# Attention with hashed masks, a gated product layer and eight experts on one core: key parts, row writes, a weight split and gates in other places

## The chip, the cores and the metric

The kernel runs on one core of a Trainium2 chip. The core has five engines, each with its own queue of instructions, worked off in order: TensorE (PE in the rows, its weight loads PEld), VectorE (DVE), ScalarE (ACT), GpSimd (POOL) and SyncE (SP, which here only issues transfers). They wait for each other by semaphores. The metric is device microseconds (us) of one execution; less is better.

## The reference

Three layers follow one another. The attention (2 batches, 8 heads, 768 rows, head width 64) lets a query see only keys of its own bucket, where a bucket is the six signs of a projection; the gated layer multiplies two products of its input and maps them back; the last layer sends each row to the one expert of eight with the largest logit.

```python
q_bits = (np.einsum('bhsd,dk->bhsk', q, proj) > 0).astype(np.int64)
k_bits = (np.einsum('bhsd,dk->bhsk', k, proj) > 0).astype(np.int64)
mask = q_bucket[:, :, :, None] == k_bucket[:, :, None, :]
scores = np.where(mask, scale * np.matmul(q, k.transpose(0, 1, 3, 2)), -1000000000.0)
attn = softmax(scores); x = np.matmul(attn, v)          # then rows of 512, 1536 of them
y = (x @ w_a) * (x @ w_b) @ w_out                       # 512 -> 1536 -> 512
xn = y / (np.linalg.norm(y, axis=-1, keepdims=True) + 1e-06)
logits = xn @ en.T / tau; expert_idx = np.argmax(logits, axis=1)
out[mask] = gate_w[mask, None] * (np.maximum(y[mask] @ w1[e], 0.0) @ w2[e])   # for each e
```

## The kernel before

Everything is written in the order in which it is to run; each engine gets its share of that order, and nothing is sorted anew afterwards.

**Attention** (`attention`, from L70). Work goes in 48 units of 256 query rows of one head, three to a head; two heads share their tiles (a pair). In a unit TensorE makes two score tiles (`st`, L205 and the masks' part L208), VectorE takes the row maximum (`nm`, L213), ScalarE exponentiates (`e`, L219), GpSimd scales (L232), VectorE transposes in blocks (`et`, L239). The first two units of a head, s = 0 and 1, each do half of the value products of the head two before it (`pv`, L248), into four banks (`pvb`), two for each half of the rows. In the third, s = 2, these banks are emptied by ScalarE (`xp`, `co`, L268) and are then used for the next pair: in one kind of head for the transposes of raw keys and queries (`turned`, L114), which ScalarE copies out (`k`, `q`, L128), in the other kind for their projections (`signs`, L163 and L181), of which ScalarE takes the signs (`sk`, `qf`, L154). From the key signs two masks are made (`kf`, L143, by `masks`). Both kinds fill the key's banks in the middle of the unit (`fresh`) and the query's at its end. The functions that empty them are kept in `preps` and called in the next unit, behind its first exponential and behind `masks()`. The value products of that next unit write the same banks.

Weight steps of the gated layer are hung into units by a table (`plan`, `places`): each of six jobs has seven steps, among them a GpSimd addition (L465), a VectorE guard (`late`, L476) and a last split into a rounded part (ScalarE, L481) and its rest (GpSimd, L482).

**Gated layer and router.** From there on there is one list, `main`, of TensorE's pieces: `p` are six products of the gated layer (`ab`, L551), after the last of four of which VectorE multiplies (`a`, L564), ScalarE rounds (`g`, L565) and GpSimd takes the rest (L566); `o` are six products back (`yp`, L583), whose sums VectorE adds into `y` (L588). `after` hangs a job behind a named piece, `chain` a list of jobs behind successive pieces. L is the last of the six chunks of that layer; the pieces of its groups 0 and 1 feed the first batch (rows 0 to 5 of twelve), of groups 2 and 3 the second.

The router's steps are such jobs. `route_in` (T) writes a row block of `y` out (`ybuf`, L646, from SyncE), squares it (`sq`, L653) and transposes it (`yt`, L656). `group_logits` (GL) makes the logits of three blocks (`lgt`, copied by ScalarE to `lgs`, L686), `group_turn` (GT) turns them (`lgu`, L694). The tile of `lgs` and that of the squares are the same single buffer. `route_norm` (`nrm`), `route_choose` (L715 to L729), `route_places` (`pos`, L737), `route_slots` (`slots`, L774) and `gather` (L838) find and fetch the rows of each expert; `route_gates` (VectorE L792 to L802, with an exponential on ScalarE, L793) and `route_gate_slots` (`gates`, L809) give the weights. ScalarE loads a table before that exponential and before the square root of `nrm`.

The experts' weights come by `fetch_expert` and are split by `split_expert` into a rounded part (ScalarE, L832) and its rest (GpSimd or VectorE, L833). `transpose_in` (`xgt`, L854) turns gathered rows; `hidden_rows` (`hr`, L895), `hidden_turn` (`ht`, L910) and `expert_out` (`op`, L927) are the first expert's products. The small products of the router and all transposes there share two banks (`rt`).

Of the kernel before, what the change touches and what calls it, by code (L numbers as in the profile page):

```python
# [25 lines left out]
class Kernel:  # L26
# [37 lines left out]
    def attention(self, xh, xl, pools, hook):  # L64
        nc = self.nc
# [237 lines left out]
        preps = signs(0, 1), signs(0, 0)  # L303
# [4 lines left out]
        preps = []  # L308
# [6 lines left out]
        for u in range(NU + 2):  # L315
            i, r = divmod(u, 6)
            s, w = u % 3, u - 2
            act, last, tr = u < NU, 0 <= u - 1 < NU, w >= 0
            done, fin = divmod(u - 11, 6) if u >= 11 else (-1, 0)
            new = len(pairs)  # L320
            if u == 1 or s == 2 and r == 5:
                new, kind = 1 if u == 1 else (u + 7) // 6, turned
            elif u == 3 or s == 2 and u > 2:
                new, kind = 1 if u == 3 else i + 1, signs
            fresh = []
            if act:
                rowmax(u, 0)
                scores(u, 1)
            moves = [((u - 8) // 3, g) for g in (1, 0)] if s == 2 and u >= 8 else []
            for m in moves[:2 if u == NU - 1 else 1]:  # L330
                epilogue(*m)
            if moves and new < len(pairs):
                fresh.append(kind(new, 1))
            if act:
                expo(u, 0)
            for m in moves[2 if u == NU - 1 else 1:]:
                epilogue(*m)
            masks()
            for prep in preps:
                prep(nc.scalar)  # L340
            if preps and held_kind is turned and held + 1 < len(pairs):
                load(held + 1)
            preps = []
            if u + 1 < NU:
                scores(u + 1, 0)
            if last:
                recip(u - 1)
                normal(u - 1)
            if tr:
                turn(w, 0)  # L350
            hook(u, 3)
            if act:
                rowmax(u, 1)
            if tr:
                turn(w, 1)
            if act:
                expo(u, 1)
            if new < len(pairs):
                preps, held, held_kind = fresh + [kind(new, x) for x in (1, 0)[len(fresh):]], new, kind
            elif s < 2 and u >= 6:  # L360
                pv((u - 6) // 3, range(12 * s, 12 * s + 12))
            hook(u, 0)
            if s == 1 and u >= 7 and (u - 1) // 3 < 2 * len(pairs):
                load_v((u - 1) // 3)
            hook(u, 1)
            if done == len(pairs) - 2:
                for g in range(3):
                    if fin == 2:
                        finish_add(done, cols[g])
            else:  # L370
                for start, step, args in finish:
                    done, fin = divmod(u - 11 - start, 6)
                    if fin == 0 and 0 <= done < len(pairs) - 2:
                        step(done, *args)
            hook(u, 4)
# [39 lines left out]
class Experts:  # L415
# [226 lines left out]
    def route_in(self, i):  # L642

        nc = self.nc
        b, c = divmod(i, self.TB)
        nc.sync.dma_start(  # L646
            out=self.ybuf[b].rearrange("(p c) d -> p c d", c=self.TB)[:, c], in_=self.y[:, i]
        )
        if c == 0:
            self.ss[b] = self.small("ssq", [128, self.TB])  # L650
            self.lg[b] = self.small("lg", [128, self.TB, self.E])
        sq = self.sb.tile([128, self.DM], F32, tag="sq", name="sq", bufs=1)
        nc.scalar.activation(sq, self.y[:, i], AF.Square, accum_out=self.ss[b][:, c:c + 1])  # L653
        p = self.rt.tile([128, 512], F32, tag="rt", name="yt")
        for k in range(self.KD):
            nc.tensor.transpose(p[:, k * 128:(k + 1) * 128], self.y[:, i, k * 128:(k + 1) * 128], self.K.ident)  # L656
        t, c = divmod(i, 3)
        if c == 0:
            self.yT[t] = self.sb.tile([128, self.KD, 384], F32, tag="yt", name="yt", bufs=1)
        nc.vector.tensor_copy(  # L660
            self.yT[t][:, :, c * 128:(c + 1) * 128], p.rearrange("p (k s) -> p k s", s=128)
        )
# [383 lines left out]
def tile_kernel(ctx, tc, q, k, v, proj, w_a, w_b, w_out, emb, tau, w1, w2, out, dbg=None):  # L1046
    K = Kernel(tc, q, k, v, proj, w_a, w_b, w_out, emb, tau, w1, w2, out)
    nc = tc.nc
# [3 lines left out]
    with tc.manual_schedule():  # L1052
# [15 lines left out]
        with tc.tile_pool(name="conv", bufs=1, side="left") as X.conv, \  # L1068
                tc.tile_pool(name="att", bufs=2, side="right") as sb, \
                tc.tile_pool(name="ps_s", bufs=2, space=PSUM) as ps_s, \  # L1070
                tc.tile_pool(name="ps_pv", bufs=1, space=PSUM) as ps_pv:

            def spare():
                return X.mid.tile([128, 4 * 384], F32R, tag="g", name="spare")

            def late():
                return sb.tile([128, 2 * S], F32, tag="raw", name="late", bufs=1)

            jobs = [X.load_first(w, f, spare) for f in range(2) for w in range(2)]
            outs = [X.load_first(2, f, late) for f in range(2)]  # L1080


            plan = {(-1, 0): [jobs[0][0], jobs[1][0]], (37, 1): [outs[0][0]], (47, 1): [outs[1][0]]}
            places = (
                (3, 4, 5, 6, 6, 9, 12), (7, 10, 11, 12, 12, 13, 18), (15, 17, 19, 22, 22, 23, 28), (21, 25, 26, 28, 28, 29, 34),
                (42, 43, 43, 44, 44, 44, 45),
            )
            plan[NU + 2, 3] = outs[1][1][:4]
            plan[NU + 2, 4] = outs[1][1][4:6]
            plan[NU + 3, 3] = outs[1][1][6:]  # L1090
            for (_, steps), us in zip(jobs + outs, places):
                for m, u in enumerate(us):
                    plan.setdefault((u, 3 if m in (3, 4, 6) else 4), []).append(steps[m])
            plan[13, 0], plan[19, 0] = [jobs[2][0]], [jobs[3][0]]
            first = [(t, f, w, h) for t in range(2) for f in range(2) for w in range(2) for h in range(2)]


            fill = {41: 2, 44: 2, NU: 2, NU + 2: 2, NU + 3: 2, NU + 4: 6}

            held = []  # L1100

            def hook(u, at):
                if at == 3:
                    while held:
                        held.pop(0)()
                for job in plan.pop((u, at), []):
                    job()
                if at == 0:
                    for n in range(fill.get(u, 0)):
                        t, f, w, half = first.pop(0)  # L1110
                        if half == 0:
                            X.part = K.banks[(2, 0)[n // 2]] if u < NU else K.bank()
                        X.gated_products(0, t, f, w, half, X.part, held if u < NU else None)

            K.attention(X.xh, X.xl, (sb, ps_s, ps_pv), hook)
            assert not plan and not first
# [15 lines left out]
        def after(name, fn, *args):  # L1132
            side.setdefault(name, []).append(lambda: fn(*args))

        def chain(name, jobs, stride=1):

            at = next(i for i, m in enumerate(main) if m[0] == name)
            for job in jobs:
                if job:
                    for fn, *args in (job if isinstance(job, list) else [job]):  # L1140
                        after(main[at][0], fn, *args)
                at += stride
# [69 lines left out]
        L = NCH - 1  # L1212
        after(("p", L, 0, 0, 0, 0), reopen)
        for n in range(4):
            after(("p", L, 1 + n // 2, n % 2, 0, 0), split, 0, n, G)
        after(("p", L, 3, 0, 0, 0), split, 0, 4, G)
        after(("o", L, 2, 1), split, 0, 5, G)
        after(("o", L, 2, 2), split, 0, 6, G)
        after(("o", L, 3, 2), split, 0, 7, G)
        after(("e", 0, 1, 0), X.transpose_in, 1, 0)  # L1220
        after(("e", 0, 1, 1), X.transpose_in, 1, 1)
        for n, at in enumerate((("t", 0, 1, 1), ("e", 0, 1, 1), ("e", 0, 1, 2), ("e", 0, 1, 3))):
# [9 lines left out]
        def begin():  # L1232
# [7 lines left out]
        chain(("o", L, 0, 2), [(T, 0), (T, 1), (T, 2), (GL, 0), (GT, 0)], 2)  # L1240
        chain(("o", L, 1, 2), [
            (T, 3), (T, 4), [(T, 5), (X.route_norm, 0)], (GL, 1), [(GT, 1), (X.route_choose, 0)],
            None, None, None, (X.route_places, 0), None, [(X.route_slots, 0), (X.gather, 0, 0)],
            (X.route_gates, 0), None, None, None, None, None, (X.route_gate_slots, 0),
        ])
        chain(("o", L, 2, 1), [(T, 6), (T, 7), (T, 8), (GL, 2), (GT, 2)])
        after(("p", L, 3, 1, 1, 1), begin)
        after(("o", L, 3, 0), X.transpose_in, 0, 0)
        after(("o", L, 3, 0), X.gather, 1, 0)
# [5 lines left out]
        after(("h", 0, 1, 0), X.route_gates, 1)  # L1255
        after(("e", 0, 0, "half"), X.transpose_in, 0, 1)
        after(("e", 0, 0, 2), X.gather, 1, 1)
        after(("e", 0, 1, 0), X.route_gate_slots, 1)
        after(("h", 1, 0), X.route_most)
        for e in range(2, X.E):  # L1260
            for b in range(B):
# [44 lines left out]
```

## Time and profile before

| | before |
|---|---|
| median of 3 runs | 738.83 us (737.4 to 739.58) |
| profiled execution | 740.01 us |
| its span, first to last instruction | 738.1 us |
| TensorE busy | 706.0 us (96%) |
| VectorE, ScalarE, GpSimd busy | 458.5, 356.7, 441.7 us |
| granted TensorE clock, mean | 0.994 |
| chain that ended last, TensorE's share | 79% |

The attention fills the span up to about 240 us, the gated layer follows up to about 537 us, with the router among its last 50, and the experts fill the rest. A timeline row gives the start and the length in microseconds, the engine, the line of the program and the operation; square brackets at its end give how long the engine was idle just before it and which operation's end released it.

### The profile page before, as it was taken

What the parts mean: (1) busy time and instruction counts of PE and PEld (TensorE: products, weight loads), DVE (VectorE), ACT (ScalarE), POOL (GpSimd) and SP (SyncE); (2) the same over time, 40 slices, a digit from 0 to 9 for tenths busy, and PEclk for the clock granted to TensorE, in tenths of its full rate; (3) what the DMA queues carried; (4) which work ended last, traced back from release to release, by engine and by line L of the source; (5) the groups of instructions that cost most, each with busy time, mean ns of one, the idle gap of its engine ahead of it and who ended that gap; (6) DMA issues with size and microseconds to landing.
All of it is one profiled execution on the core that took longest, in us unless ns stands there. A gap on an engine that the chain in (4) does not pass through costs nothing.

```text
span 738.1 us, 16439 instructions
## 1 busy us (share of the span) xinstructions
PE 706.0 (96%) x6793; PEld 584.3 (79%) x6793; DVE 458.5 (62%) x669; ACT 356.7 (48%) x657; POOL 441.7 (60%) x453
## 2 busy tenths in 40 slices
PE   7799999999989999999999999999999999999996
PEld 4356555555658999999999999998888999889995
DVE  3888988988885654655545536434744855555650
ACT  4677887877674333221221221234436655556551
POOL 1666998988786472662745646634513866556651
PEclk9899999999999999999999999999999999999999
DMA  6954566456233230230311111254250957666510
GB/s 151 189 122 111 135 153 140 93 116 138 50 76 108 76 121 27 63 109 6 110 58 58 57 58 58 105 168 155 66 178 30 293 197 241 222 217 239 208 61 23
DMA packets 68605, 88.31 MB, mean 120 GB/s; under 512 B 28963, under 2 KB 41123, under 8 KB 68528
## 3 DMA queue, kind: packets, MB, share of 16 engines
q1 hardware_dynamic: 64320, 79.49, 37.8%
q0 software_dynamic: 2560, 7.34, 2.6%
q8 instruction: 54, 0.88, 0.5%
q10 hardware_dynamic: 1648, 0.39, 0.3%
q14 instruction: 23, 0.19, 0.1%
HBM read 75.52 MB, written 7.34 MB: 112 GB/s over the span
## 4 chain that ended last, share of the span: by engine, by line
PE 79%; DVE 5%; ACT 5%; issue 4%; DMA 3%; POOL 3%; SPq 0%; POOLq 0%; DVEq 0%; ACTq 0%
PE ab L551 24%; PE yp L583 13%; PE op L927 10%; PE hp L877 9%; PE pv L248 8%; PE st L205 5%; ACT e L219 2%; DVE nm L213 2%; PE part L551 2%; PE hr L895 2%; DMA vr<-in_v_dram 2%; DVE et L239 1%; PE st L208 1%; PE xgt L854 1%; POOL e L232 1%
## 5 line engine op out<-in xcount | busy, mean ns | idle before, releaser
L551 PE MATMUL ab<-xh,w 128*128 128x384 f32 x704 | 185.8, 338 | 0.0
L551 PEld LDWEIGHTS ab<-xh,w 128*128 128x128 f32 x704 | 127.7, 188 | 2.0 <-issue 1.2
L566 POOL TENSOR_TENSOR g<-a,g 128x384 fp32r<-128x384 f32 x48 | 57.2, 1191 | 105.8 <-ACT g L565 105.7
L551 PE MATMUL ab<-xl,w 128*128 128x384 f32 x352 | 118.3, 336 | 0.0
L833 POOL TENSOR_TENSOR w<-raw,w 128x1024 fp32r<-128x1024 f32 x36 | 88.0, 2448 | 33.8 <-ACT w L832 32.7
L219 ACT ACTIVATE e<-st,nm 128x768 f32<-128x768 f32 x96 | 86.5, 902 | 40.8 <-DVE nm L213 20.3
L213 DVE TENSOR_REDUCE nm<-st 128x1 f32<-128x768 f32 x96 | 90.2, 941 | 22.7 <-PE st L208 22.6
L583 PE MATMUL yp<-w,g 128*128 128x512 f32 x432 | 102.9, 390 | 0.0
L232 POOL TENSOR_SCALAR e<-e,s,mc 128x768 f32<-128x768 f32 x96 | 95.0, 998 | 5.4 <-POOL s L230 0.2
L239 DVE STREAM_TRANSPOSE et<-e 128x768 f32<-128x768 f32 x96 | 92.3, 963 | 3.9 <-issue 1.5
L205 PE MATMUL st<-ks,qs 64*128 64x384 f32 x192 | 86.5, 531 | 8.2 <-ACT e L219 7.7
L205 PE MATMUL st<-k,q 64*128 64x384 f32 x192 | 86.6, 532 | 7.9 <-ACT e L219 6.9
L583 PEld LDWEIGHTS yp<-w,g 128*128 128x128 f32 x432 | 80.4, 188 | 14.9
L927 PE MATMUL op<-w,hth 128*128 128x512 f32 x256 | 81.0, 397 | 0.1
L877 PE MATMUL hp<-xgh,w 128*128 128x256 f32 x448 | 80.7, 281 | 0.0
L565 ACT CAST g<-a 128x384 fp32r<-128x384 f32 x48 | 24.7, 515 | 104.9 <-DVE a L564 104.9
L248 PE MATMUL pv<-et,vr 32*64 32x192 f32 x3072 | 71.4, 325 | 3.9 <-ACT q L128 1.6
L248 PEld LDWEIGHTS pv<-et,vr 32*64 32x64 f32 x3072 | 59.8, 130 | 19.4 <-issue 9.7
L833 DVE TENSOR_TENSOR w<-raw,w 128x1024 fp32r<-128x1024 f32 x28 | 64.6, 2308 | 14.9 <-ACT w L832 14.9
L877 PEld LDWEIGHTS hp<-xgh,w 128*128 128x128 f32 x448 | 69.1, 188 | 0.3
L560 ACT COPY a<-ab 128x384 f32<-128x384 f32 x44 | 21.0, 478 | 95.1 <-PE ab L551 93.7
L551 PEld LDWEIGHTS ab<-xl,w 128*128 128x128 f32 x352 | 66.2, 188 | 0.8
(202 smaller groups left out, 1244.3 us busy)
## 6 DMA issues: line engine op xcount, KB each, us to landing
raw<-in_moe_w_dram SPq DMA_DIRECT2D x32, 1024.0 KB, 5.3
vr<-in_v_dram SPq DMA_DIRECT2D x64, 192.0 KB, 4.3
raw<-in_moe_w_a_dram SPq DMA_DIRECT2D x5, 1024.0 KB, 5.1
raw<-in_moe_w_b_dram SPq DMA_DIRECT2D x5, 1024.0 KB, 5.0
raw<-in_moe_w_out_dram SPq DMA_DIRECT2D x5, 1024.0 KB, 5.0
raw<-in_k_dram SPq DMA_DIRECT2D x16, 192.0 KB, 4.7
qs<-q SPq DMA_DIRECT2D x16, 192.0 KB, 3.1
ybuf<-y SPq DMA_DIRECT2D x12, 256.0 KB, 6.1
```

The costliest lines, as they stand in the source:

```text
L205: nc.tensor.matmul(st[:, n, :H2], q[d, ql], k[d], start=True, stop=False, tile_position=(64 * n, 0))
L213: nc.vector.tensor_reduce(NM[u][:, t:t + 1], ST[u, t][:, :, :H2], axis=AX.XY, op=ALU.max, negate=True)
L219: nc.scalar.activation(e, ST.pop((u, t))[:, :, :H2], AF.Exp, bias=NM[u][:, t:t + 1], accum_out=SU[u][:, t:t + 1])
L232: nc.gpsimd.tensor_scalar(E[u, t], E[u, t], r[:, t:t + 1], c[:, t:t + 1], ALU.mult, ALU.add)
L239: nc.vector.transpose(ET[h][:, :, c], E.pop((u, t)).rearrange("p a (b s) -> p (a b) s", s=32))
L248: nc.tensor.matmul(pvb[a // 2][m:m + 64, a % 2, :NC * 32], v[d], et[d, n].rearrange("p c s -> p (c s)"), start=(n < 2), stop=(n >= NB32 - ...
L551: nc.tensor.matmul(p[:, :384], w[:, k, fs], x[:, k, cols], start=(k == 0 and n == 0), stop=(k == self.KD - 1 and n == 2),)
L566: nc.gpsimd.tensor_tensor(gl[:, f], a, f32(gh[:, f]), ALU.subtract)
L583: nc.tensor.matmul(p, g[:, f, rows], w[:, f], start=(n == 0), stop=(n == 5))
L833: eng.tensor_tensor(l, raw, f32(h), ALU.subtract)
L877: nc.tensor.matmul(p[:, :256], w[:, k, fs], x[:, k], start=(n == 0), stop=(n == 3 * self.KD - 1))
L927: nc.tensor.matmul(p, h[:, 2 * n + f, rows], w[:, f], start=(n == 0 and f == 0 and m == 0), stop=(n == 3 and f == 1 and m == 2),)
```

## The change

Seven edits, none of which changes what is computed. The functions that empty the key's banks are called at the end of their own unit, behind its second exponential, where they were called in the next unit together with the query's. The row blocks 9 to 11 are written from ScalarE's queue. In the table of weight steps the guard and the last split of the fifth job stand one unit later. The split of expert 0's piece 4 stands behind the last `p` piece of the layer, seven pieces later. Slots, the gather and the gates of the first batch stand one piece later, and so does the turning of the logits of group 2. The gate slots of the second batch stand ahead of the transpose that shares their place.

```diff
             if new < len(pairs):
-                preps, held, held_kind = fresh + [kind(new, x) for x in (1, 0)[len(fresh):]], new, kind
+                for prep in fresh:
+                    prep(nc.scalar)
+                preps, held, held_kind = [kind(new, x) for x in (1, 0)[len(fresh):]], new, kind
...
         b, c = divmod(i, self.TB)
-        nc.sync.dma_start(
+        (nc.scalar if i >= 2 * self.TB - 3 else nc.sync).dma_start(
...
-                (42, 43, 43, 44, 44, 44, 45),
+                (42, 43, 43, 44, 44, 45, 46),
...
-        after(("p", L, 3, 0, 0, 0), split, 0, 4, G)
+        after(("p", L, 3, 1, 1, 1), split, 0, 4, G)
...
+        after(("e", 0, 1, 0), X.route_gate_slots, 1)
         after(("e", 0, 1, 0), X.transpose_in, 1, 0)
...
-            None, None, None, (X.route_places, 0), None, [(X.route_slots, 0), (X.gather, 0, 0)],
-            (X.route_gates, 0), None, None, None, None, None, (X.route_gate_slots, 0),
+            None, None, None, (X.route_places, 0), None, None, [(X.route_slots, 0), (X.gather, 0, 0)],
+            (X.route_gates, 0), None, None, None, None, (X.route_gate_slots, 0),
         ])
-        chain(("o", L, 2, 1), [(T, 6), (T, 7), (T, 8), (GL, 2), (GT, 2)])
+        chain(("o", L, 2, 1), [(T, 6), (T, 7), (T, 8), (GL, 2), None, (GT, 2)])
...
-        after(("e", 0, 1, 0), X.route_gate_slots, 1)
```

On ScalarE, where a head's third unit passes into the next head's first (the first cycle with signs), the order was this; `e` is an exponential, `sk` and `qf` the key and query signs, `kf` the two masks:

```order
L219 ACTIVATE e,su<-st,nm 128x768
L268 COPY xp<-pv 64x2x6x32
L268 COPY co<-pv 64x2x6x32
L219 ACTIVATE e,su<-st,nm 128x768 x2
L154 ACTIVATE sk<-pv,bias 128x384
L154 ACTIVATE qf<-pv,bias 128x384
L219 ACTIVATE e,su<-st,nm 128x768 x2
L143 ACTIVATE kf<-sk,fac 128x384 x2
```

And now:

```order
L219 ACTIVATE e,su<-st,nm 128x768
L268 COPY xp<-pv 64x2x6x32
L268 COPY co<-pv 64x2x6x32
L219 ACTIVATE e,su<-st,nm 128x768
L154 ACTIVATE sk<-pv,bias 128x384
L219 ACTIVATE e,su<-st,nm 128x768
L143 ACTIVATE kf<-sk,fac 128x384 x2
L154 ACTIVATE qf<-pv,bias 128x384
```

The key signs moved ahead of the next unit's first exponential, and with them the masks, which that unit calls ahead of its query signs.

On VectorE, at the gates of the first batch (`so` ends the slots, `lg` to `th` are the gates, `y` the sums of rows 6 and 7), the order was:

```order
L786 CAST so<-oif 128x8
L792 TENSOR_TENSOR lg<-lg,mx 128x48
L795 TENSOR_REDUCE gt<-lg 128x6
L796 TENSOR_SCALAR gt<-gt 128x6
L797 RECIPROCAL gt<-gt 128x6
L799 TENSOR_TENSOR tg<-oh,gt 128x48
L801 CAST th<-tg 128x6x8
L802 TENSOR_TENSOR th<-tg,th 128x6x8
L564 TENSOR_TENSOR a<-ab,a 128x384
L588 TENSOR_TENSOR y<-yp,y 128x512 x2
```

And now:

```order
L788 CAST so<-oif 128x8
L566 TENSOR_TENSOR a<-ab,a 128x384
L794 TENSOR_TENSOR lg<-lg,mx 128x48
L797 TENSOR_REDUCE gt<-lg 128x6
L798 TENSOR_SCALAR gt<-gt 128x6
L799 RECIPROCAL gt<-gt 128x6
L801 TENSOR_TENSOR tg<-oh,gt 128x48
L803 CAST th<-tg 128x6x8
L804 TENSOR_TENSOR th<-tg,th 128x6x8
L590 TENSOR_TENSOR y<-yp,y 128x512 x2
```

The gates now stand between the layer's last product `a` and the sums; on ScalarE their table load and exponential likewise moved behind the rounding of that product and behind the moved split's rounding.

On TensorE, at the logits of group 2 (`lgt`, turned by `lgu`; `hr` are the first hidden products), the order was:

```order
L684 MATMUL lgt<-yt,enT 32x384 x4
L656 MATMUL yt<-ident,y 128x128 x4
L583 MATMUL yp<-w,g 128x512 x6
L694 MATMUL lgu<-ident,lgs 128x128 x3
L656 MATMUL yt<-ident,y 128x128 x4
L672 MATMUL lgp<-enT,yt 128x8 x4
L895 MATMUL hr<-w,xgh 128x256 x8
L895 MATMUL hr<-w,xgl 128x256 x4
```

And now:

```order
L686 MATMUL lgt<-yt,enT 32x384 x4
L658 MATMUL yt<-ident,y 128x128 x4
L585 MATMUL yp<-w,g 128x512 x6
L658 MATMUL yt<-ident,y 128x128 x4
L674 MATMUL lgp<-enT,yt 128x8 x4
L897 MATMUL hr<-w,xgh 128x256 x8
L897 MATMUL hr<-w,xgl 128x256 x4
L696 MATMUL lgu<-ident,lgs 128x128 x3
```

The turning moved behind the first hidden products, so that `lgs`, whose buffer the next square uses, is read there.

## Rows read from the trace of the kernel before

**Rows 1.** Busy time by stretch: us, PE, PEld, DVE, ACT, POOL (instructions), PEclk, DMA.
```profile
140.00:180.00 40.00, 37.51 (x722) 21.89 (x720) 34.60 (x48) 30.77 (x65) 34.30 (x59) 1.00 0.54 120
520.00:560.00 40.00, 39.76 (x275) 35.46 (x275) 21.95 (x77) 18.39 (x34) 14.22 (x10) 1.00 0.41 124
```

**Rows 2.** The chain of waits, start, length, engine and line, a copy cycle.
```profile
117.92 0.70 ACT k L128
```

**Rows 3.** The timeline of ScalarE, cycles with signs.
```profile
129.39 0.66 ACT L460 ACTIVATE r<-spare 128x512 int32<-128x512 uint32 x1
...
130.82 0.58 ACT L154 ACTIVATE sk<-pv,bias 128x384 bf16<-128x384 f32 x1
131.28 0.59 ACT L154 ACTIVATE qf<-pv,bias 128x384 bf16<-128x384 f32 x1
...
134.33 1.11 ACT L143 ACTIVATE kf<-sk,fac 128x384 bf16<-128x384 bf16 x2
...
155.85 0.90 ACT L219 ACTIVATE e<-st,nm 128x768 f32<-128x768 f32 x1 [0.36 <-DVE r L223]
```

**Rows 4.** The timeline of TensorE, value products behind copies and behind signs.
```profile
119.38 2.21 PE L248 MATMUL pv<-et,vr 32*64 32x192 f32 x96 [0.32 <-ACT q L128]
...
131.98 2.21 PE L248 MATMUL pv<-et,vr 32*64 32x192 f32 x96
```

**Rows 5.** The timeline of VectorE, the guard in unit 44.
```profile
207.54 1.21 DVE L476 SCALAR_TENSOR_TENSOR late<-late 128x512 f32<-128x512 f32 x1 [1.09 <-POOL late L465]
```

**Rows 6.** The timeline of all engines, first choice; last row, the second slots.
```profile
516.20 2.40 POOL L833 TENSOR_TENSOR w<-raw,w 128x1024 fp32r<-128x1024 f32 x1
...
516.34 2.32 DVE L721 TENSOR_TENSOR eq<-eq,em 128x48 f32<-128x48 f32 x1
...
519.20 0.20 PE L737 MATMUL pos<-ohb,tri 128*128 128x56 bf16 x1 [0.76 <-DVE ohb L727]
...
521.56 1.10 PE L774 MATMUL slots<-tl,sel 128*128 128x16 f32 x6
...
548.70 0.73 PE L774 MATMUL slots<-tl,sel 128*128 128x16 f32 x6
```

**Rows 7.** The timeline of all engines, gates of the first batch to row 6.
```profile
522.31 1.28 ACT L793 ACT_TABLE_LOAD   x1
...
524.70 2.89 PE L583 MATMUL yp<-w,g 128*128 128x512 f32 x12
...
525.19 0.55 DVE L564 TENSOR_TENSOR a<-ab,a 128x384 f32<-128x384 f32 x1
...
526.19 1.05 ACT L832 CAST w<-raw 128x1024 fp32r<-128x1024 f32 x1
526.26 0.69 DVE L588 TENSOR_TENSOR y<-yp,y 128x512 f32<-128x512 f32 x1 [0.52 <-PE yp L583]
...
527.36 4.74 POOL L833 TENSOR_TENSOR w<-raw,w 128x1024 fp32r<-128x1024 f32 x2
527.42 0.60 PE L656 MATMUL yt<-ident,y 128*128 128x128 f32 x4
```

**Rows 8.** The timeline of all engines, second logits to second place products.
```profile
537.22 0.63 ACT L653 ACTIVATE sq<-y 128x512 f32<-128x512 f32 x1 [1.78 <-PE lgu L694]
...
540.17 0.60 PE L656 MATMUL yt<-ident,y 128*128 128x128 f32 x4
...
543.90 0.17 DVE L675 COPY lg<-lgp 128x8 f32<-128x8 f32 x1 [1.36 <-PE lgp L672]
...
545.64 0.19 PE L737 MATMUL pos<-ohb,tri 128*128 128x56 bf16 x1
```

**Rows 9.** The timeline of SyncE's queue, one row block written.
```profile
490.38 0.35 SPq L646 DMA_DIRECT2D ybuf<-y  x1
```

**Rows 10.** The timeline of TensorE behind the second gates.
```profile
564.34 0.66 PE L910 MATMUL ht<-ident,hs 128*128 128x128 f32 x4 [0.89 <-DVE xgl L858]
```

**Rows 11.** Busy time by stretch, columns as in the first group, early attention.
```profile
26.00:28.00 2.00, 2.00 (x8) 0.76 (x10) 1.82 (x4) 0.99 (x2) 1.83 (x4) 0.50 1.08 211
```

## The prediction

> **What bounds the kernel now.** I read the page's engine table, the busy time by stretch, the chain of waits, and then the timelines of single engines at the places that the change touches. In the second half TensorE is the bound: in 520 to 560 us it is busy 39.76 of 40 us [rows 1], so whatever makes it wait there is added to the end. In the attention no engine is full: TensorE is busy 37.51 of 40 us and VectorE 34.60 [rows 1], and a cycle of three units (one head) goes round a ring: ScalarE empties the banks, TensorE multiplies, VectorE takes the maximum, ScalarE exponentiates. The chain of waits in such a cycle holds the key copy, 0.70 us [rows 2], with the query copy behind it; the value products start when the query part is out of its bank (TensorE idle 0.32 us, released by the query copy; in the other kind of cycle the query signs end at 131.28 + 0.59 = 131.87 and the products start at 131.98) [rows 3, 4]. From the value products on TensorE works without a break to the end of their second half, and the next cycle starts from there. So what moves the start of the value products moves the end.
>
> **Key parts in their own unit, the six cycles with signs.** Before, ScalarE did: exponential, key signs, query signs, and the two masks in the unit after. Now: key signs, exponential, both masks, query signs. The masks were harmless where they stood; now they stand ahead of the query signs, for which TensorE waits. Steps by the starts of successive rows [rows 3]: key signs 131.28 - 130.82 = 0.46; two masks 1.01 (the row's 1.11 less 0.1 by which neighbouring rows overlap). In five of the six cycles ScalarE idles 0.36 before that exponential [rows 3], so it moves by 0.46 - 0.36 = 0.10, and the query signs by 0.10 + 1.01 - 0.46 = 0.65. In the sixth a weight step (129.39) fills the gap: 0.46 + 0.55 = 1.0. Sum 5 x 0.65 + 1.0 = 4.25; I take off 0.5, an estimate, for cycles in which VectorE's nearly full queue (34.60 of 40 us) [rows 1] would have been late anyway: **+3.7**. Bounds: 0, if VectorE's queue set the cycle, and 6 x 1.0 = 6.
>
> **The five cycles with copies.** The query copy loses the key copy ahead of it (0.70) but its exponential is pushed by what the idle time before it doesn't cover [rows 2]. TensorE gets back at most the 0.32 that it waits for the copy [rows 4]; where the gap is small the later exponential holds up the score products instead. I take a fourth of that: **-0.4** (from -1.6, five times 0.32, to +0.7, one whole key copy).
>
> **Weight step in units 44 to 46.** VectorE waits 1.09 for GpSimd and then works 1.21 [rows 5], ahead of a maximum; a unit later the wait is gone, but the work stands ahead of the next maximum. **-0.2** (-1.1 to +0.2).
>
> **Router, the split taken away from the first choice.** A choice operation of VectorE lasts 2.32 and ends with GpSimd's 2.40 split that began just before it (518.66 and 518.60); TensorE's place products wait 0.76 for that [rows 6]. With the split moved away the 0.76 go; the slots, one place later, no longer run 1.10 behind their selectors but about 0.73 as the second time, 0.37 less [rows 6]. TensorE comes 1.13 earlier to what follows.
>
> **The gates one place later.** This is the largest term. ScalarE's table load and exponential for the gates stood ahead of the last rounding of a product; now they stand behind it and behind the moved split's rounding. And on VectorE the seven gate operations stand ahead of the sums for rows 6 and 7, as before, but later. Working it out [rows 7]: the last products end at 524.70 - 1.13 = 523.57; VectorE's product and ScalarE's rounding take 525.19 to 526.19, 1.00, so the split's rounding starts at 524.6; it takes 1.05 (525.65), the table load 1.28 (526.9), exponential and gate operations 1.6 (from the load's end, 523.59, to 525.19): 528.5. The sum of row 6 takes 0.69: 529.2. But GpSimd now runs two splits back to back from 525.7, 4.74 in all, to 530.5, and by the choice operation of rows 6 a two-input operation on small VectorE tiles stands still as long as such a split runs; the last gate operation is of that form, so it is done at about 531.0 and the sum at 531.7. TensorE has the transposes of row 6 next at 527.42 - 1.13 = 526.3 and waits there; everything behind starts 531.7 - 527.42 = **+4.3** late (the 1.13 are in it). Bounds: +1.8 without the standstill; -1.1 if TensorE never waited.
> [...]
>
> **Logits of group 2 one place later.** The turned logits' products now stand behind the first hidden products, about where a transpose begins at 540.17. But ScalarE's square of row 9 shares its buffer with them and waits for them already (1.78 idle, starts 537.22) [rows 8]; it would start at about 540.1, 2.9 later. Behind it on ScalarE stand a split's rounding, two squares, a table load and the norm; two of the moved row writes are issued there as well, 0.7 by SyncE's issue of such a row, 0.35 [rows 9]. VectorE has 1.36 of idle time ahead of the last logits that the norm is multiplied with (543.90) [rows 8]. So the second choice, and with it the place products that now run at 545.64 without waiting, come 2.9 + 0.7 - 1.4 - 0.6 (an estimate for what TensorE gains by not waiting for the turned logits) = **+1.6** late. Bounds +0.8 to +2.9. The writes cost nothing more: the gather that reads them waits for the slots, which stand behind those place products.
>
> **Gates of expert 0's second half ahead of the transpose.** TensorE waits 0.89 for VectorE to empty one of two banks [rows 10]. With the gates first the bank it needs next is the gates', emptied by two short operations: **-0.9** (-0.9 to 0).
>
> **Sum.** 3.7 - 0.4 - 0.2 + 4.3 + 1.6 - 0.9 = +8.1. The profiled execution took 740.01 (span 738.1), 1.18 more than the median of 738.83; what is added is the same for both, so 738.83 + 8.1 = 746.9.
>
> **Rivals.**
> 1. TensorE's clock falls in the long wait. [...] Against it: in the two later stretches of rows 1 TensorE idles too, in shorter pieces, and keeps 1.00. [...]
> 2. GpSimd doesn't hold VectorE up (the gate operations slip between the splits, or are not of the kind that stops): 4.3 becomes 1.8, 744.4.
> 3. VectorE's queue sets the attention's cycle (busy 34.60 of 40), so the later query signs cost nothing: 3.7 becomes about 0: 743.2. Against it: it idles wherever TensorE's scores come late.
> 4. No slower: what ScalarE does late in the router isn't waited for. This takes that the sum of row 6 is there by 526.3 and the second choice by 545.4. Then 4.3 becomes -1.1 and 1.6 becomes 0: 8.1 - 5.4 - 1.6 = +1.1, 739.9, no change that can be told. For it: TensorE has six product banks to run ahead in; against it: the transposes stand in its own queue, ahead of the products that could fill the time. With the attention's delay hidden as well the waits removed would show, and it would be 736.
>
> **How the numbers follow.** The forecast 0.45 (its own range 745 to 748.5), rival 1 0.20, rival 2 0.14, rival 3 0.08, rival 4 0.08 for no change and 0.05 for its faster end. The range from 741 to 750 leaves out most of rival 4 and the upper bounds added together. A measurement of this kernel tells about 0.3%, 2.2 us, from no change; so slower 0.86, the same 0.09, faster 0.05.
>
> **What would show it.** In the profile after: the query signs behind two masks, and the value products starting 0.65 later after the exponential in six cycles; TensorE's transposes of row 6 with an idle time of some 5 us released by a VectorE sum, and the gate operations on VectorE lasting up to the end of GpSimd's splits; the place products of the second choice with 1 to 2 us of idle time; no idle time before the slots, the first place products and the transposes after the second gates. Wrong would be: the row 6 transposes within 1 us of the products ahead of them, or attention cycles of the old length.

## The result and the profile after

The changed kernel takes 746.76 us (746.54 to 746.92, 5 runs) where the kernel before takes 738.83: a ratio of 1.0107 (95% interval 1.0092 to 1.0122). It is slower, by 7.93 us; predicted were 8.1, that is 746.9. The profiled execution is one of 746.76 us, span 745.0 [rows 1 to 11 are of one with 738.1].

The two traces are best laid side by side by landmarks of TensorE, whose work is the same in both: the start of a named group of matmuls in each, and the stretch from one to the next (us).

| from the landmark before to | before | after | difference | predicted |
|---|---|---|---|---|
| second half of the first head's value products | 45.55 | 44.08 | -1.47 | none |
| last head but one, first half of its value products (220.05, 220.66) | 174.50 | 176.58 | +2.08 | +3.1 |
| first `yp` behind the attention (243.57, 243.75) | 23.52 | 23.09 | -0.43 | 0 |
| first choice's place products (519.20, 519.05) | 275.63 | 275.30 | -0.33 | -0.76 |
| transposes of row 6 (527.42, 532.59) | 8.22 | 13.54 | +5.32 | +5.06 |
| transposes of row 7 (529.25, 536.07) | 1.83 | 3.48 | +1.65 | 0 (rival 1: later) |
| second choice's place products (545.64, 553.71) | 16.39 | 17.64 | +1.25 | +1.6 |
| first products `hp` of the next expert (569.41, 576.65) | 23.77 | 22.94 | -0.83 | -0.9 |
| last matmul (731.43, 738.25) | 162.02 | 161.60 | -0.42 | 0 |

The differences add up to +6.82, as the last matmul does (738.25 - 731.43). The profiled execution of before stood 1.18 above its median, that of after on it: 746.76 - 740.01 + 1.18 = 7.93. The 5.06 is the prediction's 4.3 and the 0.76 that it counted as gained ahead of the place products.

By stretch (us, then busy PE, PEld, DVE, ACT, POOL, then the granted clock and DMA), after:

```profile
140.00:180.00 40.00, 37.06 (x720) 21.73 (x720) 34.84 (x48) 30.53 (x64) 33.49 (x58) 1.00 0.50 120
520.00:560.00 40.00, 33.35 (x218) 29.20 (x217) 22.30 (x69) 15.67 (x29) 14.55 (x9) 0.91 0.34 107
530.00:535.00 5.00, 2.41 (x8) 2.12 (x9) 3.76 (x6) 2.28 (x5) 2.10 (x2) 0.50 0.41 104
```

In the second stretch TensorE was busy 39.76 of 40 us before [rows 1]; now it is 33.35, and the clock granted to it there is 0.91. The third line says where: in 530 to 535 it is 0.50.

The gates of the first batch, timeline of all engines (start, length, engine, line, output<-input; in brackets the idle time before and what ended it):

```profile
526.52 1.28 ACT L795 ACT_TABLE_LOAD   x1
526.62 4.79 POOL L835 TENSOR_TENSOR w<-raw,w 128x1024 fp32r<-128x1024 f32 x2
...
528.33 0.66 DVE L798 TENSOR_SCALAR gt<-gt 128x6 f32<-128x6 f32 x1
529.02 0.19 DVE L799 RECIPROCAL gt<-gt 128x6 f32<-128x6 f32 x1
529.25 2.22 DVE L801 TENSOR_TENSOR tg<-oh,gt 128x48 f32<-128x48 f32 x1
531.51 0.19 DVE L803 CAST th<-tg 128x48 fp32r<-128x48 f32 x1
...
531.85 1.28 DVE L590 TENSOR_TENSOR y<-yp,y 128x512 f32<-128x512 f32 x2
...
532.59 1.11 PE L658 MATMUL yt<-ident,y 128*128 128x128 f32 x4 [5.51 <-DVE y L590]
...
533.36 2.90 PE L585 MATMUL yp<-w,g 128*128 128x512 f32 x6
...
536.07 0.63 PE L658 MATMUL yt<-ident,y 128*128 128x128 f32 x4
```

These answer to [rows 7]; two more rows of the trace before belong beside them:

```profile
524.60 0.21 DVE L799 TENSOR_TENSOR tg<-oh,gt 128x48 f32<-128x48 f32 x1
...
527.78 1.64 PE L583 MATMUL yp<-w,g 128*128 128x512 f32 x6
```

The product of choice and gate, `tg`, took 0.21 us before and takes 2.22; it ends at 531.47, and GpSimd's two splits at 531.41. TensorE stands for 5.51. Behind that wait the same four transposes take 1.11 for 0.60 and the products `yp` 2.90 for 1.64.

The first choice after, timeline of all engines [rows 6]:

```profile
517.10 0.21 DVE L723 TENSOR_TENSOR eq<-eq,em 128x48 f32<-128x48 f32 x1
519.05 0.20 PE L739 MATMUL pos<-ohb,tri 128*128 128x56 bf16 x1
...
522.45 0.73 PE L776 MATMUL slots<-tl,sel 128*128 128x16 f32 x6
```

The choice operation is down from 2.32 to 0.21, the place products wait for nothing, and the slots take 0.73 for 1.10. The cycle with signs in which a weight step (`r`) stands ahead of the exponential, timeline of ScalarE and TensorE [rows 3, 4]:

```profile
128.47 0.57 ACT L154 ACTIVATE sk<-pv,bias 128x384 bf16<-128x384 f32 x1
128.93 0.67 ACT L462 ACTIVATE r<-spare 128x512 int32<-128x512 uint32 x1
129.50 0.89 ACT L219 ACTIVATE e<-st,nm 128x768 f32<-128x768 f32 x1
...
130.38 1.11 ACT L143 ACTIVATE kf<-sk,fac 128x384 bf16<-128x384 bf16 x2
131.39 0.57 ACT L154 ACTIVATE qf<-pv,bias 128x384 bf16<-128x384 f32 x1
...
132.01 2.21 PE L248 MATMUL pv<-et,vr 32*64 32x192 f32 x96 [0.40 <-ACT qf L154]
```

One of the five without a weight step, the cycle of the last row of [rows 3]:

```profile
155.14 0.57 ACT L154 ACTIVATE sk<-pv,bias 128x384 bf16<-128x384 f32 x1
155.60 0.90 ACT L219 ACTIVATE e<-st,nm 128x768 f32<-128x768 f32 x1
...
157.50 0.57 ACT L154 ACTIVATE qf<-pv,bias 128x384 bf16<-128x384 f32 x1
...
158.12 2.21 PE L248 MATMUL pv<-et,vr 32*64 32x192 f32 x96 [0.40 <-ACT qf L154]
```

The masks `kf` stand ahead of the query signs `qf`, and TensorE's value products wait 0.40 for these; before they waited for nothing in this kind of cycle. The guard on VectorE [rows 5] runs without its wait of 1.09:

```profile
212.48 0.85 DVE L478 SCALAR_TENSOR_TENSOR late<-late 128x512 f32<-128x512 f32 x1
```

The logits and the second gates [rows 8 to 10] after:

```profile
541.88 0.36 ACTq L648 DMA_DIRECT2D ybuf<-y  x1
...
546.82 0.63 ACT L655 ACTIVATE sq<-y 128x512 f32<-128x512 f32 x1 [4.54 <-PE lgu L696]
...
552.29 0.63 PE L912 MATMUL ht<-ident,hs 128*128 128x128 f32 x4 [0.35 <-DVE lg L677]
553.71 0.19 PE L739 MATMUL pos<-ohb,tri 128*128 128x56 bf16 x1 [0.79 <-DVE ohb L729]
...
571.60 0.63 PE L912 MATMUL ht<-ident,hs 128*128 128x128 f32 x4
```

The square waits for the turned logits 4.54 in place of 1.78, and TensorE then waits 0.35 and 0.79 where it did not wait before. What it no longer waits for is small, as a row of the trace before shows:

```profile
537.75 1.06 PE L672 MATMUL lgp<-enT,yt 128*128 128x8 f32 x8 [0.18 <-DVE lg L696]
```

Behind the second gates its wait of 0.89 is gone.

### The profile page after: what moved, and what is told of

The parts are those of the page before. It is cut to its first block, busy times and chain, and to the rows that moved or that the text cites. A ratio compares the mean times of both kernels' runs of the same rounds, so it can differ in the third digit from the quotient of the medians.

```text
span 745.0 us, 16437 instructions
## 1 busy us (share of the span) xinstructions
PE 706.1 (95%) x6793; PEld 585.1 (79%) x6793; DVE 460.3 (62%) x669; ACT 355.9 (48%) x657; POOL 439.7 (59%) x453
## 3 DMA queue, kind: packets, MB, share of 16 engines
q10 hardware_dynamic: 2080, 1.18, 0.5%
## 4 chain that ended last, share of the span: by engine, by line
PE 78%; ACT 7%; DVE 6%; issue 4%; DMA 2%; POOL 1%; SPq 0%; POOLq 0%; DVEq 0%; ACTq 0%
PE ab L553 24%; PE yp L585 12%; PE op L929 10%; PE hp L879 10%; PE pv L248 9%; PE st L205 5%; ACT e L219 3%; DVE nm L213 3%; PE part L553 2%; DVE et L239 1%; PE hr L897 1%; PE st L208 1%; PE xgt L856 1%; DMA vr<-in_v_dram 1%; PE yt L658 1%
## 5 line engine op out<-in xcount | busy, mean ns | idle before, releaser
L568 POOL TENSOR_TENSOR g<-a,g 128x384 fp32r<-128x384 f32 x48 | 55.0, 1146 | 107.4 <-ACT g L567 107.4
L585 PE MATMUL yp<-w,g 128*128 128x512 f32 x432 | 104.5, 394 | 0.3 <-POOL g L568 0.3
```

Of the source, the lines that this page charges most:

```text
L568: nc.gpsimd.tensor_tensor(gl[:, f], a, f32(gh[:, f]), ALU.subtract)
L585: nc.tensor.matmul(p, g[:, f, rows], w[:, f], start=(n == 0), stop=(n == 5))
```

## The experiments

Each was timed beside the kernel before on its chip, where that took 737.6 to 738.1 in the median. The changed kernel itself, timed once more, gave 746.9 us, ratio 1.0129 (1.0112 to 1.0146), above the 1.009 to 1.012 that were expected: its own time is the same, the kernel before beside it took 738.09, and the loss is then 8.8 us in place of 7.9. The kernel before varies by 4 us from run to run, so where an edit is worth 1 or 2 us the stretches of the table decide and the ratio only has to agree.

**The gates back in their place.**

```diff
-    None, None, None, (X.route_places, 0), None, None, [(X.route_slots, 0), (X.gather, 0, 0)],
-    (X.route_gates, 0), None, None, None, None, (X.route_gate_slots, 0),
+    None, None, None, (X.route_places, 0), None, [(X.route_slots, 0), (X.gather, 0, 0)],
+    (X.route_gates, 0), None, None, None, None, None, (X.route_gate_slots, 0),
```

> The changed kernel with the slots and gates of the first batch back in their old places (slots, gather and gates each one place earlier); the split stays moved. In the changed kernel TensorE waits 5.51 us for the sum of row 6, and its next transposes start 1.65 later still, in a stretch at a granted clock of 0.50. Theory: both come from the place of the gates on ScalarE. Then the wait goes, the granted clock stays at 1.00 in 525 to 545, the slots give back 0.37: 746.8 - 5.5 - 1.65 + 0.4 = 740.0. Rival: the clock falls for another reason and stays low: 741.7. Rival: the gates are not what delays row 6, and the time stays above 744.

739.4 us, ratio 1.0021 (1.0008 to 1.0035). Place products to row 6 take 8.41 (13.54), row 6 to row 7 1.83 (3.48), and the granted clock in 525 to 545 is 1.00. So 5.13 + 1.65 = 6.8 us of the loss belong to this edit.

**One split fewer beside the gates.**

```diff
-    after(("o", L, 2, 1), split, 0, 5, G)
+    after(("o", L, 2, 2), split, 0, 5, G)
```

> The changed kernel with the splitting of weight piece 5 of the first expert one place later, so that GpSimd runs one split beside the gates and not two in a row. Nothing ahead of the gate operations changes on ScalarE or VectorE. Theory (a two-input operation of VectorE stands still while a GpSimd split runs): the product of choice and gate, 2.22 us in the changed kernel, takes about 0.21, the sums of rows 6 and 7 and the transposes come about 2.0 earlier, and the wait of TensorE falls from 5.5 to about 3.5: 744.8, and 743.1 if the clock then stays up. Rival (ScalarE's lateness alone makes the wait, the operation is long for another reason): the operation stays at 2.2 us and the time at 746.8.

745.03 us, ratio 1.0102 (1.0085 to 1.0118). The ratio can't tell it from the changed kernel; the timeline of all engines does:

```profile
526.02 2.34 POOL L835 TENSOR_TENSOR w<-raw,w 128x1024 fp32r<-128x1024 f32 x1
...
528.65 0.21 DVE L801 TENSOR_TENSOR tg<-oh,gt 128x48 f32<-128x48 f32 x1
...
529.98 1.12 PE L658 MATMUL yt<-ident,y 128*128 128x128 f32 x4 [3.50 <-DVE y L590]
```

The operation that stood still takes 0.21 for 2.22, and the wait falls by 2.01 to the 3.50 that were expected: the standstill is 2.0 of the 5.5. Behind 3.50 us the clock falls as well (granted 0.72 in 530 to 535; row 6 to row 7 take 3.19).

**TensorE busy in the wait.**

```diff
+        for k in range(36 if i == 6 else 0):
+            nc.tensor.transpose(p[:, k % 4 * 128:(k % 4 + 1) * 128], self.K.ident, self.K.ident)
```

> The changed kernel with 36 more transposes of the identity into the bank of row 6, ahead of its own transposes, so that TensorE works through most of the wait of 5.5 us. They add nothing to the output. Theory (the 1.65 us behind the wait are the clock, which falls because TensorE stood still): the granted clock stays at 1.00 in 530 to 540, the product behind the transposes takes 1.63 and not 2.90, and the time falls to about 745.2. Rival (the products behind the wait are slow for another reason, the splits or the load of the next weights): they stay at 2.9 and the time stays at 746.8 or above.

744.29 us, ratio 1.0091 (1.0073 to 1.011). The timeline of TensorE, and the line of a stretch of 5 us:

```profile
525.95 4.09 PE L658 MATMUL yt<-ident 128*128 128x128 f32 x36
...
531.64 0.66 PE L660 MATMUL yt<-ident,y 128*128 128x128 f32 x4 [1.60 <-DVE y L590]
...
532.05 1.64 PE L585 MATMUL yp<-w,g 128*128 128x512 f32 x6
```

```profile
530.00:535.00 5.00, 3.40 (x20) 2.88 (x20) 4.08 (x8) 2.78 (x6) 2.10 (x2) 1.00 0.63 150
```

Row 6 comes no sooner, and the splits beside it are the same; but the clock stays at 1.00, the products take 1.64, and row 6 to row 7 take 1.88. So the 1.65 are the clock's, and the rival that another engine slows these products is out. In the second trace of the changed kernel the low clock reaches further into the work (the mean over 525 to 545 is 0.83 in both traces), row 6 to row 7 taking 3.47, and row 7 to row 8 3.05 (1.85 in the first): 2.8 us. The execution was no longer for it, since its start-up was 1.4 shorter (below). Over the five traces with a wait of 5.51 the two stretches from row 6 to row 8 are together 1.3 to 2.9 longer than before.

**The turned logits back in their place.**

```diff
-    chain(("o", L, 2, 1), [(T, 6), (T, 7), (T, 8), (GL, 2), None, (GT, 2)])
+    chain(("o", L, 2, 1), [(T, 6), (T, 7), (T, 8), (GL, 2), (GT, 2)])
```

> The changed kernel with the turning of the logits of rows 6 to 8 back one place earlier. My prediction gave this edit +1.6; the trace of the changed kernel shows the second choice's place products, from the transposes that follow the fall of the clock, another 1.25 late, with two waits of 0.35 and 0.79. Theory: undoing it gives back about 1.2: 745.6. Rival: what is late at the second choice is late from the gates anyway (ScalarE's splits and squares are queued behind them), so undoing it gives nothing, 746.8, and the wait moves to TensorE's turning.

744.96 us, ratio 1.0105 (1.0085 to 1.0125). Row 7 to the second place products take 16.42, as before (16.39), and not 17.64; these products wait for nothing. So the edit costs 1.2, and what is late from the gates doesn't hide it. The row writes still go out from ScalarE here: they cost nothing beyond that 0.03.

**The key parts back, and the masks alone back.**

```diff
-                for prep in fresh:
-                    prep(nc.scalar)
-                preps, held, held_kind = [kind(new, x) for x in (1, 0)[len(fresh):]], new, kind
+                preps, held, held_kind = fresh + [kind(new, x) for x in (1, 0)[len(fresh):]], new, kind
```

> The changed kernel with the key parts moved back into the next unit, all else as changed. Theory (the masks, 1.0 us, stand ahead of the query signs, and TensorE waits for these): in each of the six cycles with signs TensorE's wait of 0.40 for the query signs goes, and the stretch from the second half of the second head's value products (44.08) to the first products behind the attention (243.75) gets shorter by 1.5 to 3 us: ratio to the kernel before 1.007 to 1.0085 where the changed kernel had 1.0107. Rival (VectorE's nearly full queue sets the cycle): the stretch stays within 0.5 us and the ratio at 1.0107.

```diff
-            masks()
+            if not preps:
+                masks()
```

> The changed kernel with the key parts in their own unit as changed, but the two masks left where they stood before, one unit after the query signs. Tells the two halves of that edit apart. Theory (the masks ahead of the query signs are the whole cost): it is as fast as or faster than the kernel with the key parts moved back; the query signs run about 1.0 us earlier in a cycle with signs than in the changed kernel and TensorE's wait of 0.40 for them goes: six times 0.4 to 0.6, a ratio of 1.007 to 1.0075. Rival (the key signs pushing the exponential are the cost, and then the transpose of VectorE): the stretch stays as long as in the changed kernel, and the ratio at 1.0107.

744.51 us, ratio 1.0095 (1.0074 to 1.0116), and 744.96 us, ratio 1.0096 (1.0079 to 1.0113). From the first landmark of the table to the second the changed kernel takes 176.58 (176.57 in its second trace), with the key parts back 174.28, with the masks alone back 173.98. The stretch got shorter by 2.3, as expected (1.5 to 3), and by 2.6. Both ratios missed what was expected (1.007 to 1.0085 and 1.007 to 1.0075); that was worked out from 1.0107, and beside the 1.0129 of the second timing they are 0.003 lower, about 2.5 us. The timeline of ScalarE and TensorE with the masks alone back, again in the cycle with the weight step:

```profile
127.77 0.57 ACT L154 ACTIVATE sk<-pv,bias 128x384 bf16<-128x384 f32 x1
128.80 0.90 ACT L219 ACTIVATE e<-st,nm 128x768 f32<-128x768 f32 x1
...
129.68 0.58 ACT L154 ACTIVATE qf<-pv,bias 128x384 bf16<-128x384 f32 x1
...
130.85 2.21 PE L248 MATMUL pv<-et,vr 32*64 32x192 f32 x96
```

The query signs follow the exponential and the wait of 0.40 is gone. So the masks ahead of the query signs make the cost: cycle by cycle, the changed kernel (second trace) is longer than this one by 0.46 to 0.47 in each of the six cycles with signs. The key signs one unit earlier cost 0.48 in this one cycle, where the weight step left no idle time ahead of the exponential (this kernel against the one with the key parts back), and the five cycles with copies give back 0.75: a gain of 0.3 in all.

**The edits that gained, alone.** The split moved, the second gates first, and the slots one place later with the gates directly behind them, on the kernel before; and the same with the key parts moved and the masks left:

```diff
-    None, None, None, (X.route_places, 0), None, [(X.route_slots, 0), (X.gather, 0, 0)],
-    (X.route_gates, 0), None, None, None, None, None, (X.route_gate_slots, 0),
+    None, None, None, (X.route_places, 0), None, None, [(X.route_slots, 0), (X.gather, 0, 0), (X.route_gates, 0)],
+    None, None, None, None, None, (X.route_gate_slots, 0),
```

> The kernel before with three of the edits of the router alone: the split moved away from the first choice, the slots and the gather one place later (the gates stay at their old place, directly behind), and the second gates ahead of the transpose. By the prediction's terms these are gains: the wait of 0.76 for the place products, 0.37 of the slots and the 0.89 of the second transposes: 2.0 less than the kernel before, ratio 0.9973. Rival (the split, moved, holds up the gate operations or their sum at the new place as it did the choice): row 6 waits for about 1 to 2 us and the ratio is 0.999 to 1.0005.

> The kernel of the three router edits with the key parts in their own unit and the masks left one unit after the query signs. Theory (that half of the edit is harmless or a small gain, since the copy cycles come 0.1 to 0.7 earlier): 0 to 2 us less than with the router edits alone, ratio 0.995 to 0.9975, faster than both kernels. Rival (the key parts one unit earlier cost something of their own): ratio above that of the router edits alone, by 1 to 2 us.

736.02 us, ratio 0.9989 (0.9971 to 1.0008), and 737.03 us, ratio 0.9993 (0.9978 to 1.0007). In their traces the stretch to the first place products is 274.71 and 274.70 (275.63 before): the 0.76 are gained, and 0.16 more. No wait stands at row 6. From the second choice to the next expert the second takes 22.94, as the changed kernel does; the first 23.64, since another wait came there, on the gather:

```profile
550.04 0.63 PE L854 MATMUL xgt<-ident,xg 128*128 128x128 f32 x4 [0.72 <-DMA xg<-ybuf,gi]
```

Neither interval told them from the kernel before, and the ratio expected of the second (0.995 to 0.9975) was missed, so it was timed again beside the changed kernel:

> The changed kernel as it is, timed once more beside the kernel before and the next kernel, since the kernel before varies by 4 us from run to run there, together with its mean granted clock. Expected: ratio 1.009 to 1.012, and in its trace the same stretches behind the attention as in its first trace: 13.5 us from the first choice's place products to the transposes of row 6, and 3.5 to those of row 7.

> The kernel of the three router edits and the key parts in their own unit with the masks left a unit after the query signs, timed once more: by its trace it is 3.0 us shorter than the kernel before from the second products of the first head to the end (682.86 to 685.88), but its first interval, 0.9978 to 1.0007, doesn't tell it from the kernel before. Theory: the 3.0 us are real and the spread is the clock of the start-up: ratio 0.996 to 0.998. Rival: the trace was a lucky one: 0.999 to 1.001.

736.91 us, ratio 0.999 (0.9973 to 1.0006): faster than the changed kernel by 10 us, but not told from the kernel before, and spread from 733.62 to 741.54. The median is the rival's; only the trace (683.4 us from the first landmark to the last matmul, 682.9 in its first, 685.9 before) speaks for a gain.

**The start-up's clock.** The first line of the table moved by 1.47 though nothing is changed ahead of it. By stretch, 24 to 40 us of the kernel before:

```profile
24.00:40.00 16.00, 12.65 (x58) 6.32 (x60) 13.45 (x20) 10.28 (x22) 9.80 (x18) 0.79 0.68 126
```

Here too the clock falls behind waits (of 1.27 and 0.71 in the case of [rows 11]), in this trace twice and not three times, as the expectation below has it, to 0.50 in 26 to 29 and in 37 to 39, and not in every execution: the changed kernel was granted 0.80 and 0.78 in 32 to 36 and 36 to 40 in its first trace, and 1.00 throughout in its second, where the first head's second products start at 42.72 and not at 44.08. Seven transposes at six such waits, in the kernel before and in the last kernel:

```diff
+        def busy():
+            for m in range(7):
+                nc.tensor.transpose(pvb[1][:, 0, m % 4 * 128:m % 4 * 128 + 128], self.ident, self.ident)
...
+                if u in (3, 5):
+                    busy()
...
+            if 2 <= u <= 5:
+                busy()
```

> The kernel before with six times seven more transposes of the identity into a free bank, ahead of score products that TensorE waits for in units 2 to 5 of the attention. They add nothing to the output. The kernel before takes 736 to 740 us, and its longer runs are those with a lower mean granted clock; in its trace the clock falls three times between 24 and 40 us, behind waits of 1.2 us. Theory (these falls make the spread): with the waits filled the clock stays up, all runs lie near the shortest of the kernel before, and the ratio is 0.997 to 0.999. Rival (the spread comes from elsewhere, or the transposes delay the scores by what they save): the ratio is 1.000 to 1.003 with the old spread.

> The same transposes in the kernel of the three router edits and the key parts with the masks left later. Theory: the two gains add, 2.4 to 3.0 us of its trace and 1 to 1.5 of the start-up: ratio 0.9945 to 0.997, faster than both kernels. Rival: the gain in its trace doesn't show in its median for a reason other than the clock of the start-up, and the ratio stays at 0.999.

737.6 us (736.3 to 738.4), ratio 1.0001 (0.9991 to 1.0012), and 734.99 us (734.02 to 735.96), ratio 0.9961 (0.995 to 0.9972). The same stretch of the second:

```profile
24.00:40.00 16.00, 15.60 (x107) 8.78 (x103) 14.70 (x22) 10.65 (x22) 10.00 (x18) 1.00 0.70 127
```

The clock stays at 1.00 in both, and the spread is 2 us: in place of 4 in the kernel before (735.48 to 739.47 beside them) and of 8 in the last kernel without them. The first head's second products start at 44.34 and 44.11, where they started anywhere from 42.72 to 45.68 in the twelve traces without these transposes. So most of the spread came from there. In the kernel before the transposes cost what they save, as the rival said; the expected gain (0.997 to 0.999) was missed. With most of the spread gone the other gains show: 737.6 - 735.0 = 2.6 us, as the 2.4 to 3.0 of the traces above. The traces of these two kernels alone would say 1.2 (683.85 and 682.63), since TensorE of the kernel before came 1.1 sooner from the end of the attention into the gated layer in that execution; it is the medians that tell them apart. This kernel beats both.

## Why the prediction was right

The direction and the largest term were right. That the time came within 0.2 us is luck: two errors cancelled, a loss that was left to a rival (+1.65), and terms that came out 1.0 and 0.4 too large; and the second timing puts the loss at 8.8. Point by point:

1. **Gates one place later, +4.3: right.** The chain was as worked out: rounding, table load, standstill up to the end of the splits, sums, transposes. The wait is 5.51 for 5.4; place products to row 6 +5.32 for +5.06. One link was another: not the last gate operation stood still but the product two places ahead of it, and the addition before that for a shorter time. Without the second split it is 2.0 less (the prediction's two ends lay 2.5 apart). Rival 2 is out.
2. **The clock in the wait: rival 1 happened.** It was given 0.20 and was not in the sum. It measured 1.65 in one trace and 2.8 in another (1.3 to 2.9 in all five with this wait), and keeping TensorE busy takes it away. The argument against it, that shorter pieces of idle time keep 1.00 [rows 1], said nothing about one of 5.5 us, and the fall of [rows 11], to 0.50 behind waits of 1.27 and 0.71, stood against it. In the trace after the clock is 0.50 in 530 to 535, behind 5.51 us, and 1.00 there with TensorE kept busy.
3. **Key parts, +3.7 and -0.4: direction right, the sum 1.0 too large.** Cycle by cycle, the second trace of the changed kernel against the one with the key parts back, the six cycles with signs are longer by 0.47, 0.43, 0.45, 0.94, 0.47 and 0.47, together 3.23; the prediction had five at 0.65 and one at 1.0, less 0.5. The five cycles with copies gain 0.95, not 0.4; 0.74 of it lies in one of them: 0.43 comes with the key copy's move (as with the masks alone back), the rest with the masks, which no longer stand in that cycle ahead of a weight step of ScalarE and of GpSimd's addition behind it. The 0.94 is the cycle with the weight step. The step that failed is "so it moves by 0.46 - 0.36 = 0.10, and the query signs by 0.10 + 1.01 - 0.46 = 0.65", taken as the price. Take the cycle in which the value products start at 183.40 before and at 184.01 after, and count from the start of the second half of the value products ahead of them: the exponential starts at 6.52 for 6.51, since the key signs just fill the idle time; the query signs start at 8.41 for 7.87, so 0.54 later; and the value products, which began 0.12 behind the end of the query signs and now begin 0.06 behind it, are 0.47 later.
4. **Weight step in units 44 to 46, -0.2: 0.** The 1.0 gained in one half of a head is given back in the next, 4 us on, so the trace with the edit (key parts back) and one without it (router edits alone) both take 174.3.
5. **Router's first choice, -0.76 and -0.37: right.** The wait is gone and the slots take 0.73. Of the 0.76 the first trace kept 0.33: around a wait of 0.31 for GpSimd at 266 us, which the second trace lacks, it is 0.6 longer; in the second trace the gain is 0.92 (274.71).
6. **Logits of group 2, +1.6: right in kind, measured 1.2.** The square waits 2.8 longer (4.54 for 1.78; predicted 2.9), and TensorE waits 0.79 for the second choice. The row writes, put at 0.7 within it, don't show: with the logits back in their place they cost nothing on ScalarE's queue. Nor does the estimate of 0.6 for TensorE, whose wait was 0.18. From row 7 on the norm comes 2.78 later (541.57 before, 551.17 after); 2.78 - 1.36 - 0.18 = 1.24 is what was measured: the 0.7 should have been nothing and the 0.6 less, and in part they cancelled.
7. **Second gates first, -0.9: right,** -0.83.

Rivals 3 and 4 are out: the query signs were waited for in every cycle with signs, and row 6 in full.

## What to carry to other kernels

Moving an instruction by one place moved everything queued behind it on its own engine: what the masks and the gates cost here (0.46 to 0.47 a cycle with signs, a wait of 5.51 at row 6) was paid by the query signs and the row sums behind them, not by themselves. Where a wait of a few us arises on TensorE (3.5 and 5.5 here), its own length is not the whole price, because the work behind it may run at a lower granted clock (0.50 in 530 to 535 behind 5.51; 1.3 to 2.9 us here); filling the wait with idle transposes tells the two apart. When run-to-run spread hides a gain of 0.3%, look for its place in the trace and compare stretches between landmarks, or remove the spread first.

## What was not expected of the hardware

- Which operations stood still beside a GpSimd split: the product of two SBUF tiles (128x48, 2.22 us for 0.21) and the addition of a constant to a tile of 128x6 (0.66 for 0.22, up to the end of the first split, with and without a second one behind it). Beside a shorter GpSimd operation (1.01) a comparison of two SBUF tiles took 1.02 for its 128x48 (at 516.04 in the trace after). The reduction ahead of the addition and the reciprocal behind it (0.20 and 0.19) did not stand still, nor did a sum that reads a product bank (0.69 at 527.62 in the trace before, beside the split of 527.36).
- The clock fell behind waits of TensorE of 5.5 and of 3.5 us (granted 0.50 and 0.72 in 530 to 535), and not (1.00) where 4.09 us of transposes that nobody needs left 1.60 of such a wait.
- In the start-up one program is granted 0.80 in one execution and 1.00 in another over the same 4 us (32 to 36); with the waits there filled (1.00 from 24 to 40), the runs of a kernel lie within 2 us and not 4.
